# The softmax shift from leading parts: one matmul for four heads, and two buffers for the query rows

## The chip, the cores and the metric

The kernel runs on one core of a Trainium2 chip. The metric is the device time of one execution in microseconds (us). Inputs are float32; on the matrix engine (TensorE, PE) most operands are of type fp32r, a rounded float32 that it streams faster than full float32. A value is therefore often kept as two tiles: a leading part (`h`), which is the value rounded to fp32r, and a rest (`l`), which is the value minus the leading part. The other engines are VectorE (DVE), ScalarE (ACT), GpSimd (POOL), and SyncE (SP), on whose queue nearly all DMAs are issued, in order.

## The reference

For tokens x of shape 2048 x 448, the result mixes an attention branch and an MLP branch with a gate per token:

```python
g = _sigmoid((x * gate_w).sum(-1, keepdims=True))
a = _A_ref(x, A_wq, A_wk, A_wv, A_wo)
b = _B_ref(x, B_w1, B_w2, B_w3, B_w4)
return g * a + (1 - g) * b
```

Branch A is attention with 16 heads of 28 dimensions that share one key and one value (multi-query):

```python
q = (x @ wq).reshape(B, S, H, Dh).transpose(0, 2, 1, 3)
k = x @ wk
v = x @ wv
p = _softmax(jnp.einsum("bhqd,bkd->bhqk", q, k) * (Dh ** -0.5), axis=-1)
o = jnp.einsum("bhqk,bkd->bhqd", p, v)
```

and then the projection with wo. Branch B is a layer norm, a 448 x 448 product with a gelu, shifts along the tokens, a second 448 x 448 product and a residual, and then a layer norm and an MLP of width 1792 with a second residual.

A softmax does not change when one number is taken off all the scores of a row. The kernel uses for it the row's greatest score over the first 128 keys instead of all 2048. This keeps the exponentials in range without being exact; sums above 1e12 would send the kernel into a second, slower pass under a run-time condition at its end.

## The kernel before, in words

**Stages.** The first stage (lines 219 to 376, with its loads) projects keys and values for 4 blocks of 512 tokens, and the queries of the first two units, and does the first half of branch B. The MLP stage (413 to 471) runs 4 blocks of 512 tokens over 14 tiles of the hidden width each, in a loop over `f`. The attention stage (474 on) does the rest of branch A and the gate.

**Units.** The attention goes by 16 units `u = 4 * b + g`: a block of 512 queries and a group of 4 heads. Each unit goes over 16 key tiles `kt` of 128 keys; `k` counts the key tiles of all units. For a key tile there are 4 score matmuls, one for each head (line 683), 4 exponentials (685), and, two key tiles later and for two key tiles at a time, the products with the values (`pv_group`, 645).

**What a score matmul reads.** `kS` holds in its rows 0 to 31 the leading part of the keys, in 32 to 63 the same again, in 64 to 95 their rest, and in rows 96 and on ones. The query rows `qs` hold, for each unit, the leading part of the queries (rows 0 to 31), their rest (32 to 63), the leading part again (64 to 95), and in two rows (96 and 97) the negative shift in two parts. So one matmul over 98 rows gives a score in nearly full precision less its shift.

**How the query rows come about.** A projection of four heads lies in one PSUM tile of 128 rows, row `4 * d + j` for dimension `d` of head `j`. `q_evac` (160) splits it into `qh` (ScalarE, 163) and `ql` (VectorE, 164), and three DMAs on SP (165 to 167) spread these over the rows of `qs`, so that each head has its own 512 columns. Units 0 and 1 are projected in the first stage (`stage_q`), the others by `q_job` (513), two units ahead: its job is put in front of the list at key tile 2 of unit `u - 2` (7 where that is unit 0). There are three buffers for `qs`.

**The shift.** `max_part(u, t)` (177) takes 128 queries of a unit against the first 128 keys: four matmuls of 96 rows, 128 queries and 128 keys (182), one for each head, into one PSUM tile, then one VectorE reduction over it (183). Unit `u + 1` gets its four parts at key tiles 6 to 9 of unit `u`; unit 0 gets them in the MLP stage, in a list of fills. `max_end` and `max_rows` (198, 206) turn the result into the two rows of `qs` with a transposing matmul, a ScalarE copy and two DMAs on SP. `max_full` (185) does it over all keys, for the second pass only.

**What sets the order.** TensorE's order is the order in which the program is written (line 59). The other engines' queues are ordered by a scheduler. In the attention a small pump puts one matmul of a waiting job (projection of queries, normalization, output projection) into TensorE's order after every second score matmul. A normalization job (561) needs the reciprocals of the row sums, which travel by small DMAs on SP (`rt`, 547, and `rb`, 557 and 558).

Of the kernel before, what the change touches and what calls it, by code (L numbers as in the profile page):

```python
# [8 lines left out]
F32 = mybir.dt.float32  # L9
F32R = mybir.dt.float32r  # L10
# [5 lines left out]
P = 128  # L16
# [15 lines left out]
MK = 128  # L32
# [3 lines left out]
def f32(ap):  # L36
    return ap.bitcast(F32)
# [3 lines left out]
def gated_mix_kernel(  # L41
# [13 lines left out]
    nc = tc.nc  # L55

    keep = ctx.enter_context(tc.tile_pool(name="keep", bufs=1))
# [10 lines left out]
    kS = keep.tile([P, S], F32R, name="kS")  # L68
# [4 lines left out]
    first = keep.tile([P, 4], F32, name="first")  # L73
    epst = keep.tile([P, 4], F32, name="epst")
    powt = keep.tile([P, 4], F32, name="powt")
    sel8 = keep.tile([P, P], F32R, name="sel8")
    mcs = [keep.tile([P, P], F32R, name=f"mc_{i}") for i in range(2)]
    nc.gpsimd.memset(epst, EPS)
# [2 lines left out]
    nc.gpsimd.memset(vext, 0.0)  # L81
    nc.gpsimd.memset(vext[:, :, 0:1], 1.0)
    nc.gpsimd.memset(f32(kS)[96:128, :], 1.0)
    nc.vector.tensor_add(
        sel8.rearrange("p (j d) -> p j d", j=4),
        ident[:, 0:4].unsqueeze(2).broadcast_to([P, 4, 32]),
# [36 lines left out]
    def proj32(ps, w, w3, a):  # L123
        for c in range(4):
            nc.tensor.matmul(ps, w(c) if c < 3 else w3, a[:, c, :], start=(c == 0), stop=(c == 3))
# [32 lines left out]
            split_a(tp, ah[:, :, cols], al[:, :, cols])  # L158

    def q_evac(pool, u, ps, qs):  # L160
        qh = pool.tile([P, 512], F32R, tag="qh", bufs=2 if pool.name == "s1" else 1, name=f"qh_{u}")
        ql = pool.tile([P, 512], F32R, tag="ql", bufs=2 if pool.name == "s1" else 1, name=f"ql_{u}")
        nc.scalar.copy(qh, ps)
        nc.vector.tensor_sub(ql, ps, f32(qh))
        nc.sync.dma_start(f32(qs)[0:32], f32(qh))
        nc.sync.dma_start(f32(qs)[32:64], f32(ql))
        nc.sync.dma_start(f32(qs)[64:96], f32(qh))

    NU = NB * NG
    q_of = {}  # L170
    mx_of = {}
    mc_of = {}

    def max_tile(name):
        return psA.tile([P, 512], F32, tag="mx", bufs=1, name=name)

    def max_part(u, t, tile_of):
        if t == 0:
            mx_of[u] = keep.tile([P, 4, 4], F32, tag="mr", bufs=2, name=f"mr_{u}")
        ps = tile_of(f"m_{u}_{t}").rearrange("p (j k) -> p j k", j=4)  # L180
        for j in range(4):
            nc.tensor.matmul(ps[:, j, :], q_of[u][0:96, j, t * P:(t + 1) * P], kS[0:96, 0:MK], start=True, stop=True)  # L182
        nc.vector.reduce_max(mx_of[u][:, :, t], ps, axis=AX.X)  # L183

    def max_full(u, tile_of):
# [33 lines left out]
    with tc.tile_pool(name="s1b", bufs=1) as s1b, \  # L219
            tc.tile_pool(name="ps1", bufs=1, space=PSUM) as ps1:  # L220
        s1_stack = ExitStack()
        s1 = s1_stack.enter_context(tc.tile_pool(name="s1", bufs=1))
# [45 lines left out]
        def stage_kv(b):  # L268
            cols = slice(512 * b, 512 * b + 512)
            ps = max_tile(f"kv_{b}")[0:64, :]  # L270
            if b == 0:
                proj32(ps, lambda c: kvraw[:, c, :], kvlast, xraw[0])
            else:
                ah = s1.tile([P, 4, 512], F32R, tag="ah", bufs=2, name=f"ahk_{b}")
                al = s1.tile([P, 3, 512], F32R, tag="al", bufs=2, name=f"alk_{b}")
                split_a(xraw[b], ah, al)
                proj(ps, kvh, kvl, ah, al)
            nc.scalar.copy(kS[0:32, cols], ps[0:32, :])
            nc.scalar.copy(kS[32:64, cols], ps[0:32, :])
            nc.vector.tensor_sub(kS[64:96, cols], ps[0:32, :], f32(kS)[0:32, cols])  # L280
            vT = s1b.tile([32, 512], F32, tag="vT", bufs=1, name=f"vT_{b}")
            nc.scalar.copy(vT, ps[32:64, :])
            return vT
# [9 lines left out]
        def stage_q(u):  # L293
            ps = mm_tile(f"q_{u}")
            w = slice(u * P, (u + 1) * P)
            proj32(ps, lambda c: wqraw[:, c, w], wqraw[:, 3, w], xraw[0])
            q_of[u] = keep.tile([P, 4, 512], F32R, name=f"qs_{u}", tag=f"qs{u}", bufs=1)
            q_evac(s1, u, ps, q_of[u])

        def ln1_begin(b):  # L300
            ah = s1.tile([P, 4, 512], F32R, tag="ah", bufs=2, name=f"ah1_{b}")
# [48 lines left out]
                    between(t)  # L350

        vT = stage_kv(0)
        stage_q(0)
        stage_v(0, vT)
        stage_q(1)
        ln1_begin(0)
        for t in range(4):
# [116 lines left out]
    with tc.tile_pool(name="s3", bufs=1, reuse_waits="tile") as s3, \  # L474
# [38 lines left out]
        def q_job(u):  # L513
            b, g = divmod(u, NG)
            ah, al = xact[b]
            cols = slice(g * P, (g + 1) * P)
            ps = misc_tile(f"q_{u}")
            ops = []
            for c in range(3):
                ops += [(wqh[:, c, cols], ah[:, c, :]), (wqh[:, c, cols], al[:, c, :]), (wql[:, c, cols], ah[:, c, :])]  # L520
            ops += [(wqh[:, 3, cols], ah[:, 3, :]), (wql[:, 3, cols], ah[:, 3, :])]
            for n, (w, a) in enumerate(ops):
                nc.tensor.matmul(ps, w, a, start=(n == 0), stop=(n == 10))  # L523
                if n < 10:
                    yield
            pool = keep if u % 3 < 2 else s3
            q_of[u] = pool.tile([P, 4, 512], F32R, name=f"qs_{u}", tag=f"qs{u % 3}", bufs=1)
            q_evac(s3, u, ps, q_of[u])
            yield

        rbs = [s3.tile([P, 512], F32R, name=f"rb_{i}") for i in range(2)]
# [83 lines left out]
        for n in range(NT):  # L615
            nc.gpsimd.tensor_scalar(x1[:, n, :], x1[:, n, :], gi[:, n:n + 1], None, op0=ALU.mult)

        jobs = []
        current = [None]

# [45 lines left out]
        for k in range(NU * NT + LAG):  # L666
            u, kt = divmod(k, NT)
            while delayed and delayed[0][0] <= k:
                jobs.append(delayed.pop(0)[1])
            if k == (NU - 1) * NT:  # L670
                for g in range(NG - 2):
                    for t in range(4):
                        jobs.append(lambda t=t, g=g: wo_last_job(t, g))
            if k < NU * NT:
                if kt == (7 if u == 0 else 2) and u + 2 < NU:
                    jobs.insert(0, lambda u=u: q_job(u + 2))
                if kt == 8 and (u + 3) % NG == 0 and u + 3 < NU:
                    load_x((u + 3) // NG)
                p_of[k] = []
                for j in range(4):  # L680
                    n = 4 * k + j
                    ps = s_tile(n, u == NU - 1)
                    nc.tensor.matmul(ps, kS[0:98, kt * P:(kt + 1) * P], q_of[u][0:98, j, :], start=True, stop=True)  # L683
                    p = s3.tile([P, 512], F32, tag="p", bufs=4 * (LAG + PVB) + 2, name=f"p_{n}")
                    nc.scalar.activation(p, ps, AF.Exp, scale=SCALE)  # L685
                    p_of[k].append(p)
                    if j % 2 == 1 or u == NU - 1:
                        pump()
                if u + 1 < NU:
                    if 6 <= kt < 10:  # L690
                        max_part(u + 1, kt - 6, m_tile)
                    elif kt == 10:
                        max_end(u + 1)
                    elif kt == 11:
                        max_rows(u + 1, m_tile)
            if k >= LAG and k % PVB == PVB - 1:
                for kk in range(k - LAG - PVB + 1, k - LAG + 1):
                    if kk >= 0:
                        pv_group(kk)
# [3 lines left out]
        u = NU - 1  # L703
# [50 lines left out]
        with tc.If(again > 0):  # L754
            for b in range(NB):
                load_x(b)
                for g in range(NG):
                    u = b * NG + g
                    for _ in q_job(u):
                        pass  # L760
                    max_full(u, m_tile)
                    max_end(u)
                    max_rows(u, m_tile)
                    pv = max_tile(f"pv2_{u}")
                    for kt in range(NT):
                        for j in range(4):
                            ps = mm_tile(f"s2_{u}_{kt}_{j}")
                            nc.tensor.matmul(ps, kS[0:98, kt * P:(kt + 1) * P], q_of[u][0:98, j, :],
                                             start=True, stop=True)
                            p = s3.tile([P, 512], F32, tag="p", bufs=4 * (LAG + PVB) + 2, name=f"p2_{u}_{kt}_{j}")  # L770
                            nc.scalar.activation(p, ps, AF.Exp, scale=SCALE)
                            nc.tensor.matmul(pv[32 * j:32 * j + 32, :], vext[:, kt, :], p,
                                             start=(kt == 0), stop=(kt == NT - 1), tile_position=(0, 32 * j))
                    for _ in norm_job(u, *recip_begin(u, pv, False)):
                        pass
                for t in range(4):
                    for _ in wo_job(b, t):
                        pass
# [51 lines left out]
```

## Time and profile before

| | before |
|---|---|
| median of 3 runs | 1064.49 us (1064.31 to 1066.27) |
| the profiled execution: its time | 1066.31 us |
| its span | 1064.5 us |
| TensorE busy | 1041.8 us, 98% |
| ScalarE busy | 667.3 us, 63% |
| VectorE busy | 261.7 us, 25% |
| mean granted TensorE clock | 0.992 |

In the profile, `L182` is line 182 of the kernel. PE is TensorE's matmuls, PEld its weight loads, which overlap the matmuls. A row of a group gives busy time, the mean duration of one, and the idle time of the engine just before, with what ended it (`<-`). Matmuls are pipelined, so the duration of one is longer than what it adds to a stream of them. In the chain of waits, which goes back from the last instruction to whatever released it at each step, a matmul is given with the time that it adds. A row of the chain or of a timeline begins with its start and its length in us.

### The profile page before, as it was taken

The numbers are of one execution on the slowest core, as the hardware profiler recorded it, in microseconds if no ns is written. First come the engines' busy times: TensorE is split into PE (matmuls) and PEld (weight loads), VectorE is DVE, ScalarE is ACT, GpSimd is POOL, SyncE is SP. The second block draws the span as 40 slices with busy tenths as digits, with TensorE's granted clock in tenths as the row PEclk, the third lists the DMA queues.
The fourth block names the chain that finished last, engine by engine and source line by source line (L and its number), as shares of the span: only waits on it lengthen the run. The fifth ranks groups of instructions, "written<-read, shape, count | busy, mean of one in ns | idle before, by whom it ended". The sixth has DMA issues, their size and how long they took to land.

```text
span 1064.5 us, 13873 instructions
## 1 busy us (share of the span) xinstructions
PE 1041.8 (98%) x5581; PEld 673.1 (63%) x5581; DVE 261.7 (25%) x540; ACT 667.3 (63%) x1309; POOL 132.6 (12%) x155
## 2 busy tenths in 40 slices
PE   8999899999999999999999999999999999999996
PEld 4687788888888887444554555554655555565542
DVE  6834952411412212311110110120110210111102
ACT  4444451222222224798888888888888889888873
POOL 2422200200200202502000002010002100000100
PEclk9999989999999999999999999999999999999998
DMA  9501330000000002323210202220202220211001
GB/s 306 141 1 38 113 110 1 1 1 1 1 1 1 1 1 75 119 32 71 32 22 11 36 14 40 40 31 3 39 10 41 40 32 2 39 25 26 10 2 38
DMA packets 30653, 41.21 MB, mean 39 GB/s; under 512 B 8116, under 2 KB 20212, under 8 KB 30452
## 3 DMA queue, kind: packets, MB, share of 16 engines
q1 hardware_dynamic: 30356, 40.09, 16.4%
q8 instruction: 46, 0.75, 0.3%
q14 instruction: 27, 0.22, 0.1%
q10 hardware_dynamic: 224, 0.15, 0.0%
HBM read 23.35 MB, written 3.67 MB: 25 GB/s over the span
## 4 chain that ended last, share of the span: by engine, by line
PE 93%; DVE 3%; ACT 1%; POOL 1%; DMA 1%; issue 1%; POOLq 0%; DVEq 0%; SPq 0%; ACTq 0%
PE s L683 27%; PE pv L645 22%; PE acc L439 4%; PE acc L440 4%; PE acc L441 4%; PE g L117 4%; PE g L118 4%; PE g L119 4%; PE q L523 3%; PE m L182 2%; PE wo L580 1%; PE g L121 1%; PE wo L578 1%; PE g L120 1%; PE wo L576 1%; PE h L118 1%
## 5 line engine op out<-in xcount | busy, mean ns | idle before, releaser
L685 ACT ACTIVATE p<-s 128x512 f32<-128x512 f32 x1024 | 517.6, 630 | 99.2 <-PE s L683 98.9
L683 PE MATMUL s<-qs,kS 98*128 98x512 f32 x1024 | 343.4, 420 | 1.4 <-ACT p L685 0.7
L683 PEld LDWEIGHTS s<-qs,kS 98*128 98x128 f32 x1024 | 181.6, 189 | 168.2 <-ACT p L685 127.3
L645 PE MATMUL pv<-p,vext 128*32 128x512 f32 x2048 | 247.6, 602 | 0.0
L429 ACT ACTIVATE gh<-g 128x512 fp32r<-128x512 f32 x56 | 33.5, 598 | 176.7 <-PE g L121 176.7
L645 PEld LDWEIGHTS pv<-p,vext 128*32 128x32 f32 x2048 | 53.7, 109 | 107.8 <-issue 100.4
L431 DVE TENSOR_TENSOR gl<-gf,gh 128x512 fp32r<-128x512 f32 x56 | 38.7, 692 | 185.7 <-ACT gf L430 185.6
L439 PE MATMUL acc<-w4h,gh 128*128 128x448 f32 x224 | 83.4, 372 | 0.0
L440 PE MATMUL acc<-w4l,gh 128*128 128x448 f32 x224 | 81.9, 366 | 0.0
L441 PE MATMUL acc<-w4h,gl 128*128 128x448 f32 x224 | 81.7, 365 | 0.0
L183 DVE TENSOR_REDUCE mr<-m 128x4 f32<-128x512 f32 x64 | 44.3, 691 | 147.4 <-PE m L182 146.7
L117 PE MATMUL g<-ah,w3h 128*128 128x512 f32 x168 | 67.0, 399 | 3.5 <-ACT gf L430 3.5
L119 PE MATMUL g<-ah,w3l 128*128 128x512 f32 x168 | 66.8, 398 | 0.0
L118 PE MATMUL g<-al,w3h 128*128 128x512 f32 x168 | 66.7, 397 | 0.0
L568 POOL CAST onh<-on 128x512 fp32r<-128x512 f32 x15 | 9.2, 614 | 414.4 <-DVE on L565 228.5
L541 DVE SCALAR_TENSOR_TENSOR good<-rt,good 128x16 f32<-128x16 f32 x15 | 2.6, 175 | 190.1 <-DMA rt<-o 190.1
L440 PEld LDWEIGHTS acc<-w4l,gh 128*128 128x128 f32 x224 | 42.4, 189 | 4.7
L439 PEld LDWEIGHTS acc<-w4h,gh 128*128 128x128 f32 x224 | 42.2, 189 | 4.6
L441 PEld LDWEIGHTS acc<-w4h,gl 128*128 128x128 f32 x224 | 42.2, 188 | 3.9
L182 PEld LDWEIGHTS m<-kS,qs 96*128 96x128 f32 x256 | 38.4, 191 | 6.1 <-DVE mr L183 1.2
L117 PEld LDWEIGHTS g<-ah,w3h 128*128 128x128 f32 x168 | 31.9, 190 | 9.9 <-ACT gf L430 3.9
L584 DVE SCALAR_TENSOR_TENSOR ot<-wo,gg,x 128x448 f32<-128x448 f32 x16 | 10.9, 682 | 107.7 <-PE wo L580 107.7
(200 smaller groups left out, 1101.5 us busy)
## 6 DMA issues: line engine op xcount, KB each, us to landing
qs<-qh SPq DMA_DIRECT2D x32, 256.0 KB
qs<-ql SPq DMA_DIRECT2D x16, 256.0 KB
xq<-in_xT_dram SPq DMA_DIRECT2D x4, 1024.0 KB
x<-in_x_dram SPq DMA_DIRECT2D x4, 896.0 KB
w3raw<-in_w_dram SPq DMA_DIRECT2D x7, 512.0 KB
out_dram<-ot SPq DMA_DIRECT2D x16, 224.0 KB
w4raw<-in_w_dram SPq DMA_DIRECT2D x7, 448.0 KB
xkv<-in_xT_dram SPq DMA_DIRECT2D x3, 1024.0 KB
```

Of the source, the lines that this page charges most:

```text
L117: nc.tensor.matmul(ps, wh[:, c, :], ah[:, c, :], start=(c == 0), stop=False)
L118: nc.tensor.matmul(ps, wh[:, c, :], al[:, c, :], start=False, stop=False)
L119: nc.tensor.matmul(ps, wl[:, c, :], ah[:, c, :], start=False, stop=False)
L182: nc.tensor.matmul(ps[:, j, :], q_of[u][0:96, j, t * P:(t + 1) * P], kS[0:96, 0:MK], start=True, stop=True)
L183: nc.vector.reduce_max(mx_of[u][:, :, t], ps, axis=AX.X)
L431: nc.vector.tensor_sub(gl, gf, f32(gh))
L439: nc.tensor.matmul(ps, gh[:, tok], w4h[i][:, k, :], start=(f == 0), stop=False)
L440: nc.tensor.matmul(ps, gh[:, tok], w4l[i][:, k, :], start=False, stop=False)
L441: nc.tensor.matmul(ps, gl[:, tok], w4h[i][:, k, :], start=False, stop=(f == NF - 1))
L645: nc.tensor.matmul(pv[32 * j:32 * j + 32, :], vext[:, kt, :], ps[j], start=(kt == 0), stop=(kt == NT - 1), tile_position=(0, 32 * j))
L683: nc.tensor.matmul(ps, kS[0:98, kt * P:(kt + 1) * P], q_of[u][0:98, j, :], start=True, stop=True)
L685: nc.scalar.activation(p, ps, AF.Exp, scale=SCALE)
```

## The change

The shift is taken from the leading parts of queries and keys alone. A new tile `khd` of 128 rows and 4 x 128 columns is zero but for four blocks: row `4 * d + j` holds in the columns of head `j` the leading part of dimension `d` of the first 128 keys. So `qh` itself, 128 rows by 128 queries, can be the weights of one matmul that streams 512 columns of `khd` and gives the four heads' scores at once, in the place of four matmuls from the query rows. `khd` is zeroed by GpSimd and filled by four DMAs early in the first stage.

As the parts no longer read the query rows, these are needed only when the unit begins. `q_evac` leaves the DMAs to a new `q_rows`, called at the first key tile of the unit before, and two buffers do for `qs`; `qh` gets two buffers in the attention. Unit 1's projection is copied out in full (`q1`) in the first stage, and split and spread at the start of the attention.

```diff
+    khd = keep.tile([P, 4, MK], F32R, name="khd")
+    q1 = keep.tile([P, 512], F32, name="q1")
...
+    nc.gpsimd.memset(f32(khd), 0.0)
...
     def q_evac(pool, u, ps, qs):
-        qh = pool.tile([P, 512], F32R, tag="qh", bufs=2 if pool.name == "s1" else 1, name=f"qh_{u}")
+        qh = (pool if u % 2 else keep).tile([P, 512], F32R, tag=f"qh{u % 2}", bufs=1, name=f"qh_{u}")
+        qh_of[u] = qh
         ql = pool.tile([P, 512], F32R, tag="ql", bufs=2 if pool.name == "s1" else 1, name=f"ql_{u}")
         nc.scalar.copy(qh, ps)
         nc.vector.tensor_sub(ql, ps, f32(qh))
-        nc.sync.dma_start(f32(qs)[0:32], f32(qh))
-        nc.sync.dma_start(f32(qs)[32:64], f32(ql))
-        nc.sync.dma_start(f32(qs)[64:96], f32(qh))
+        ql_of[u] = ql
+        if qs is not None:
+            q_rows(u, qs)
+
+    def q_rows(u, qs):
+        q_of[u] = qs
+        for r, src in enumerate((qh_of[u], ql_of[u], qh_of[u])):
+            nc.sync.dma_start(f32(qs)[32 * r:32 * r + 32], f32(src))
...
         ps = tile_of(f"m_{u}_{t}").rearrange("p (j k) -> p j k", j=4)
-        for j in range(4):
-            nc.tensor.matmul(ps[:, j, :], q_of[u][0:96, j, t * P:(t + 1) * P], kS[0:96, 0:MK], start=True, stop=True)
+        nc.tensor.matmul(ps, qh_of[u][:, t * P:(t + 1) * P], khd, start=True, stop=True)
         nc.vector.reduce_max(mx_of[u][:, :, t], ps, axis=AX.X)
...
-            q_of[u] = keep.tile([P, 4, 512], F32R, name=f"qs_{u}", tag=f"qs{u}", bufs=1)
-            q_evac(s1, u, ps, q_of[u])
+            if u == 0:
+                q_evac(s1, u, ps, keep.tile([P, 4, 512], F32R, name=f"qs_{u}", tag="qs0", bufs=1))
+            else:
+                nc.scalar.copy(q1, ps)
...
         vT = stage_kv(0)
+        for j in range(4):
+            nc.sync.dma_start(f32(khd)[j:P:4, j, :], f32(kS)[0:32, 0:MK])
...
-            pool = keep if u % 3 < 2 else s3
-            q_of[u] = pool.tile([P, 4, 512], F32R, name=f"qs_{u}", tag=f"qs{u % 3}", bufs=1)
-            q_evac(s3, u, ps, q_of[u])
+            q_evac(s3, u, ps, None)
...
+        def qs_tile(u):
+            return (s3 if u % 2 else keep).tile([P, 4, 512], F32R, name=f"qs_{u}", tag=f"qs{u % 2}", bufs=1)
+
+        q_evac(s3, 1, q1, qs_tile(1))
...
+                if kt == 0 and 0 < u < NU - 1:
+                    q_rows(u + 1, qs_tile(u + 1))
```

The second pass, which is not run here, gets its own call of `q_rows`.

More of the change, by code (lines that the diff above doesn't have):

```diff
@@ L164, in q_evac @@
         nc.vector.tensor_sub(ql, ps, f32(qh))
-        nc.sync.dma_start(f32(qs)[0:32], f32(qh))
-        nc.sync.dma_start(f32(qs)[32:64], f32(ql))
-        nc.sync.dma_start(f32(qs)[64:96], f32(qh))
+        ql_of[u] = ql
[5 more added lines that the diff above has]
+            nc.sync.dma_start(f32(qs)[32 * r:32 * r + 32], f32(src))
     NU = NB * NG
     q_of = {}
+    qh_of = {}
+    ql_of = {}
     mx_of = {}
@@ L760, in gated_mix_kernel @@
                         pass
+                    q_rows(u, qs_tile(u))
                     max_full(u, m_tile)
```

## The prediction

> **What bounds the kernel now.** I read the page first (busy shares, the chain that ended last), then the rows of the shift's own tile, then the chain of waits stretch by stretch through the attention.
>
> ```profile
> span 1064.5 us, 13873 instructions
> PE 1041.8 (98%) x5581; PEld 673.1 (63%) x5581; DVE 261.7 (25%) x540; ACT 667.3 (63%) x1309; POOL 132.6 (12%) x155
> ...
> PE s L683 27%; PE pv L645 22%; PE acc L439 4%; PE acc L440 4%; PE acc L441 4%; PE g L117 4%; PE g L118 4%; PE g L119 4%; PE q L523 3%; PE m L182 2%; PE wo L580 1%; PE g L121 1%; PE wo L578 1%; PE g L120 1%; PE wo L576 1%; PE h L118 1%
> ```
>
> TensorE is the bound, and the shift (L182) is itself on the chain, with 2%. What is to be seen next is how much of one attention block it takes. A block here is two key tiles: 16 pv matmuls, 8 score matmuls and whatever fills are pumped between them; it runs from one pv row to the next.
>
> ```profile
> L182 PEld LDWEIGHTS m<-kS,qs x256: 186/192/192, 159.4 to 987.8; 96*128 96x128 f32 x128
> L182 PE MATMUL m<-kS,qs x256: 222/274/328, 159.6 to 987.9; 96*128 96x128 f32 x128
> ```
>
> ```profile
> 505.50 1.85 PE pv L645 x16
> ...
> 510.37 1.85 PE pv L645 x16
> ...
> 513.60 0.23 PE q L523
> 513.83 0.40 PE m L182 x4
> ...
> 515.85 1.85 PE pv L645 x16
> ...
> 553.82 1.85 PE pv L645 x16
> ...
> 558.80 1.85 PE pv L645 x16
> ...
> 567.77 1.85 PE pv L645 x16
> 569.62 2.59 PE s L683 x8
> 572.21 1.85 PE pv L645 x16
> ...
> 625.43 1.85 PE pv L645 x16
> ...
> 631.12 1.85 PE pv L645 x16
> ...
> 636.82 1.85 PE pv L645 x16
> ...
> 641.52 1.85 PE pv L645 x16
> ```
>
> Blocks differ by their fills. With none (567.77) a block takes 4.44 us. With four q matmuls (505.50) it takes 4.87; a q matmul holds the chain for 0.235 (0.23 or 0.24 in single rows), so the block without fills would be 4.87 - 0.94 = 3.93 if TensorE alone set it. The difference, 0.51, is ScalarE:
>
> ```profile
> 565.63 4.03 ACT L685 ACTIVATE p<-s 128x512 f32<-128x512 f32 x8 [0.42 <-PE s L683]
> ```
>
> Eight exponentials take 4.03 and ScalarE waits 0.42 for the first scores, 4.45 together. So a block costs about 3.93 plus fills, and not under 4.45. Every block with shift parts has more: 5.48 (510.37: three q, two parts), 4.98 (553.82: one rbc, two parts), 5.69 (625.43: four q, two parts). There TensorE is the limit, and time taken off the shift comes off the span.
>
> **The change, part by part.**
>
> *Four matmuls become one, in the attention.* From 510.37, a part costs (5.48 - 3.93 - 3 x 0.235) / 2 = 0.42: 0.40 in its row, the rest in the scores behind it. The new matmul loads 128 x 128 weights from the qh tile and streams 512 columns of the block-diagonal tile, the very form of the q matmul: 0.235. Saved: 0.19 a part, 0.38 a block. The new block of three q and two parts is 3.93 + 5 x 0.235 = 5.10. That holds while the block stays above the floor, and one kind comes near: 553.82 becomes 3.93 + 3 x 0.235 = 4.63, where the block of three q and one short transposed row (636.82) took 4.70; I take 0.30 there (ends 0.28 and 0.35). Units 1 to 14 have two such blocks each, 28; followed along the chain, five are of the 553.82 kind and 23 have more fill: 23 x 0.38 + 5 x 0.30 = 10.2. Unit 0 has four parts, but the first ends before a wait for GpSimd (below), so three count: 0.6.
>
> The Trainium skill, page "TensorE: Matmul & The Clock Gate", section "Back-to-back issue gap", gives about 81 ns a matmul at 128 columns and 131 at 512 in a sustained stream of weight load and matmul. By those it would be 4 x 81 - 131 = 193 ns a part, an estimate beside the 0.19 from this trace; the trace's own 100 and 235 ns are what I use. The same section's formula for a lone matmul, N/2.4 + 2.5 ns, speaks against the change, since 512 columns cost the same either way; 4 x 100 against 235 in this trace disagrees with it.
>
> *The shift of unit 0, in the MLP stage.* Its four parts lie in two passes of the f loop.
>
> ```profile
> 154.21 0.60 ACT L429 ACTIVATE gh<-g 128x512 fp32r<-128x512 f32 x1 [1.84 <-PE g L121]
> 159.19 0.60 ACT L429 ACTIVATE gh<-g 128x512 fp32r<-128x512 f32 x1 [3.89 <-PE g L121]
> 165.53 0.60 ACT L429 ACTIVATE gh<-g 128x512 fp32r<-128x512 f32 x1 [5.25 <-PE g L121]
> 171.91 0.60 ACT L429 ACTIVATE gh<-g 128x512 fp32r<-128x512 f32 x1 [5.30 <-PE g L121]
> ```
>
> ```profile
> 160.91 0.69 DVE L183 TENSOR_REDUCE mr<-m 128x4 f32<-128x512 f32 x1
> ```
>
> A pass without fills is 4.98, one with two parts 6.34 and 6.38. The excess of 1.37 is two parts plus a wait: this stage has one PSUM buffer for the parts, the part at 159.6 was reduced only from 160.91, behind the subtraction gl, and the second part waited. In the changed order the first reduction stands ahead of that gl. Two new matmuls add 0.47, so 0.9 a pass, 1.8 in all; if the wait stays, 2 x 2 x 0.19 = 0.8.
>
> *The first stage.* One subtraction of q_1 on VectorE goes.
>
> ```profile
> 19.04 0.68 DVE L164 TENSOR_TENSOR ql<-q,qh 128x512 fp32r<-128x512 f32 x1
> ```
>
> ```profile
> 21.75 1.06 DVE st_s L133 x2
> ...
> 39.31 0.49 PE h L118
> ```
>
> From 21.75 to 39.31 the chain lies mostly on VectorE, so up to 0.5 of the 0.68 arrives. The scheduler also reorders VectorE there: one aggregate and statistics pair moves ahead of the al subtractions. I take 0.5 saved, with ends of 1.3 saved and 1 lost. SP issues four small loads of khd instead of three rows of qs_1, one issue more; behind them stand only the rows of unit 0, first used in the MLP stage or later. The memset of khd on GpSimd falls in its idle time there. The first load of w4 now also waits for the last kv projection, about 2.5 us later than here:
>
> ```profile
> 99.47 0.48 SPq L390 DMA_DIRECT2D w4raw<-in_w_dram  x1
> ```
>
> ```profile
> 107.36 0.92 ACT L391 CAST w4h<-w4raw 128x896 fp32r<-128x896 f32 x1
> ```
>
> Its reader starts at 107.36, so there is cover of some 8 us less the transfer and less 2.5; nothing is charged, a microsecond if the cover fails.
>
> *Start of the attention.* The split of q_1 (one copy, one subtraction, three DMAs) now stands here, and ScalarE's table load moves behind a wait for the first score.
>
> ```profile
> 432.19 3.44 POOL alq L509
> 435.67 0.50 PE q L523
> ```
>
> ```profile
> 412.77 1.28 ACT L685 ACT_TABLE_LOAD   x1
> ```
>
> ```profile
> 423.94 0.92 DVE L600 CAST wqh<-wqraw 128x768 fp32r<-128x768 f32 x1 [4.35 <-DMA wqraw<-in_wq_dram]
> ```
>
> The subtraction falls in VectorE's 4.35 us of waiting, the copy in ScalarE's pause before the scores. The late table load costs up to 1.28 at the first exponential, but TensorE stands waiting for alq until 435.67, some 3.6 us, in any case. So 0; if the cover were gone, 1.3. One of the three row DMAs is put between xq and woraw; if it slowed the loads that alq hangs on, about 1.
>
> *Query rows, moved.* Until now the three row DMAs followed the split at once; now they stand on SP at the first key tile of the unit before, waiting for that buffer's last score, ahead of rt and rb of the reciprocal.
>
> ```profile
> 454.00:455.00 1.00, 1.00 (x14) 0.26 (x8) 0.00 (x0) 1.00 (x4) 0.00 (x0) 1.00 1.12 246
> ...
> 459.00:460.00 1.00, 1.00 (x13) 0.15 (x5) 0.00 (x0) 1.00 (x3) 0.00 (x0) 1.00 0.24 27
> ```
>
> ```profile
> 503.18 0.63 SPq L547 DMA_DIRECT2D rt<-o  x1
> ```
>
> ```profile
> 505.11 0.17 DVE L541 SCALAR_TENSOR_TENSOR good<-rt,good 128x16 f32<-128x16 f32 x1 [21.05 <-DMA rt<-o]
> ```
>
> ```profile
> L558 SPq DMA_DIRECT2D rb<-rl x15: 535/557/697, 468.5 to 1012.8; - x15
> L563 PE MATMUL rbc<-rb,sel x15: 394/397/403, 480.1 to 1025.5; 128*128 128x512 f32 x15
> ```
>
> (The windows' last two columns are the DMA share and GB/s.) One unit's rows keep the DMA engines busy for some 5.2 us. Issued with the unit's first tile, they overlap the landing of rt (1.9 us today) and may delay it by 2 or 3. The first rb is issued 11.6 before its rbc matmul and the last 12.7; less a landing like rt's, 9.7 of slack. Hidden. The rows themselves have a whole unit to land.
>
> Sum: 10.2 + 0.6 + 1.8 + 0.5 = 13.1. The profiled execution took 1066.31 with its span of 1064.5, 1.8 above the median of 1064.49. Taken off the median: 1051.4.
>
> **Rivals.**
>
> *Half the gain.* The parts get shorter but their followers do not: each part's PSUM buffer needs the reduction (0.69) before the next part, or blocks fall on ScalarE's floor. Against it: the parts stand 1.6 us apart and the blocks come out above 4.6. For it: in 553.82 the margin is under 0.2. Keeping half of the 10.8: 1056.8.
>
> *Nothing gained in the attention.* The weight load of 0.19 stands bare in front of the matmul (0.19 + 0.235 = 0.42, what a part costs now), or columns alone are paid. Against it: q's loads are of the same form and hidden. Left are the wait in the MLP stage, 1.37 - 2 x 0.42 = 0.5 a pass, and the first stage's 0.5: 1.5, so 1063.0.
>
> *Slower.* The rows ahead of rt on SP delay the reciprocal past its slack and rbc stalls TensorE in 14 units. It outweighs the gain once rt lands 9.7 + 13.1 / 14 = 10.6 us late, twice what a whole set of rows takes. At 12 us late: 14 x 2.3 = 32 lost, 1083.
>
> **How the numbers follow.** Chances: forecast 0.80 (own range 1049.5 to 1053.5, from the ends of the first stage, the MLP wait and the five short blocks), half 0.12, nothing 0.04, slower 0.04. The range takes in the forecast and the half case, 1049 to 1057. Within 0.2% (2.1 us) counts as no change that a measurement can tell; the nothing case lies inside it: faster 0.92, same 0.04, slower 0.04.
>
> **What would show it.** In the new profile: a shift group of 64 matmuls at 0.235 on the chain; the three-q block at 5.1, the four-q one at 5.3, the rbc one at 4.6 to 4.7, blocks without shift unchanged; passes with parts near 5.45 in the MLP stage; alq still the wait at the start; rbc never waiting for a DMA. A new wait of the shift for its reduction, or of rbc for rb, would make the prediction wrong.

## The result and the profile after

| | before | after |
|---|---|---|
| median, run side by side | 1064.49 us (5 runs, 1062.02 to 1066.91) | 1054.31 us (5 runs, 1053.8 to 1056.95) |
| ratio after to before, 95% interval | | 0.9907 (0.9885 to 0.9928) |
| the profiled execution: its time, its span | 1066.31, 1064.5 | 1055.24, 1053.4 |
| mean granted TensorE clock in it | 0.992 | 0.991 |

The changed kernel is faster by 10.2 us. Forecast were 13.1 less, 1051.4, with a range from 1049 to 1057. So the direction, the stated range and, as will be seen, the main term were right. The narrower range that the prediction gave the forecast itself, 1049.5 to 1053.5, is missed: 2.9 us of the gain are not there. The experiments on the opening of the attention started from them.

The page of the kernel after: its span, the busy time by engine, and the chain that ended last.

```profile
span 1053.4 us, 13462 instructions
PE 1030.6 (98%) x5389; PEld 652.3 (62%) x5389; DVE 263.7 (25%) x540; ACT 667.9 (63%) x1310; POOL 132.3 (13%) x156
...
PE s L702 27%; PE pv L662 23%; PE acc L453 4%; PE acc L454 4%; PE acc L455 4%; PE g L120 4%; PE g L122 4%; PE g L121 4%; PE q L537 3%; PE m L192 1%; PE wo L592 1%; PE wo L590 1%; PE wo L588 1%; PE g L124 1%; PE g L123 1%; PE h L121 1%
```

TensorE is still the bound. There are 192 matmuls fewer, and the shift (now L192) has 1% of the chain instead of 2%. The shift's own rows, and then the chain through two places of the attention, reduced to its pv rows and one shift row (rbc is the broadcast of the reciprocals by a matmul, one of which lies in the block from 513.33):

```profile
L192 PEld LDWEIGHTS m<-khd,qh x64: 187/190/192, 160.1 to 976.0; 128*128 128x128 f32 x64
L192 PE MATMUL m<-khd,qh x64: 387/397/402, 160.3 to 976.2; 128*128 128x512 f32 x64
```

```profile
508.25 1.85 PE pv L662 x16
...
513.09 0.24 PE m L192
513.33 1.85 PE pv L662 x16
...
518.00 1.85 PE pv L662 x16
...
621.24 1.85 PE pv L662 x16
...
626.55 1.85 PE pv L662 x16
...
631.87 1.40 PE pv L662 x9
```

A part holds the chain for 0.23 to 0.24 us. The block of three q and two parts takes 513.33 - 508.25 = 5.08 us (forecast 5.10), the one with rbc 518.00 - 513.33 = 4.67 (4.6 to 4.7), those with four q 5.31 and 5.32 (5.3). From the first pv row of the block at 453.75 before, and 452.26 after, to the last pv row of the loop (1040.38 and 1028.75), before takes 586.63 us and after 576.49: 10.14 less, where units 1 to 14 were put at 10.2.

The MLP stage, by ScalarE's rows for `gh`:

```profile
159.85 0.60 ACT L443 ACTIVATE gh<-g 128x512 fp32r<-128x512 f32 x1 [3.89 <-PE g L124]
165.28 0.60 ACT L443 ACTIVATE gh<-g 128x512 fp32r<-128x512 f32 x1 [4.35 <-PE g L124]
170.75 0.60 ACT L443 ACTIVATE gh<-g 128x512 fp32r<-128x512 f32 x1 [4.39 <-PE g L124]
```

The two passes with parts take 5.43 and 5.47 (6.34 and 6.38 before): 1.82 less, forecast 1.8.

The opening of the attention is another matter. The chain of the kernel after:

```profile
418.09 0.67 ACT L704
...
420.03 5.69 PE s L702 x11
425.72 3.57 PE pv L662 x16
```

ScalarE's table load (the row `ACT L704` at 418.09) has become part of the chain, and the first 16 pv matmuls take 3.57 us instead of 1.85. The windows of four microseconds show why (columns: window; width; busy time and count of PE, PEld, DVE, ACT and POOL; granted TensorE clock; DMA share; GB/s). First after, then before:

```profile
416.00:420.00 4.00, 2.98 (x14) 2.23 (x12) 3.25 (x5) 1.90 (x3) 3.31 (x4) 1.00 0.27 51
420.00:424.00 4.00, 3.97 (x8) 1.64 (x9) 1.35 (x2) 4.00 (x9) 3.85 (x6) 0.92 0.98 358
424.00:428.00 4.00, 4.00 (x16) 1.41 (x19) 3.92 (x5) 3.33 (x7) 3.37 (x3) 0.50 0.74 181
428.00:432.00 4.00, 4.00 (x16) 1.77 (x8) 2.73 (x2) 1.94 (x5) 2.69 (x3) 0.73 0.25 27
```

```profile
420.00:424.00 4.00, 4.00 (x10) 1.53 (x9) 0.06 (x1) 4.00 (x10) 3.85 (x7) 1.00 0.93 351
...
432.00:436.00 4.00, 2.61 (x13) 1.89 (x13) 0.69 (x1) 3.98 (x8) 3.76 (x2) 1.00 0.71 226
436.00:440.00 4.00, 4.00 (x22) 1.02 (x20) 0.69 (x1) 0.04 (x1) 3.85 (x3) 0.57 0.37 116
```

After, TensorE is busy for only 2.98 of the first 4 us (the gap behind the table load), and then its clock is granted at half speed. A window of four us with a clock between 0.50 and 1.00 is read as part of a slow stretch: it holds 8 x (1 - clock) us at 0.50. So the stretch is 0.64 + 4 + 2.16 = 6.8 us long. Before, the same first scores ran at 1.00, TensorE stood at `alq` (the 2.61 of 4.00), and a shorter stretch of 8 x 0.43 = 3.4 us followed.

In the view of the opening used below, from the start of the first score matmul to the start of the sixth group of pv rows, before takes 34.91 us, after 34.58: 0.3 less, where 0.6 was forecast and the waiting for `alq` is gone as well.

### The profile page after: what moved, and what is told of

Its sections match the earlier page's. It is cut to its first block, busy times and chain, and to the rows that moved or that the text cites. A ratio compares the mean times of both kernels' runs of the same rounds, so it can differ in the third digit from the quotient of the medians.

```text
span 1053.4 us, 13462 instructions
## 1 busy us (share of the span) xinstructions
PE 1030.6 (98%) x5389; PEld 652.3 (62%) x5389; DVE 263.7 (25%) x540; ACT 667.9 (63%) x1310; POOL 132.3 (13%) x156
## 4 chain that ended last, share of the span: by engine, by line
PE 93%; DVE 3%; ACT 1%; DMA 1%; POOL 1%; issue 0%; ACTq 0%; SPq 0%; DVEq 0%; POOLq 0%
PE s L702 27%; PE pv L662 23%; PE acc L453 4%; PE acc L454 4%; PE acc L455 4%; PE g L120 4%; PE g L122 4%; PE g L121 4%; PE q L537 3%; PE m L192 1%; PE wo L592 1%; PE wo L590 1%; PE wo L588 1%; PE g L124 1%; PE g L123 1%; PE h L121 1%
## 5 line engine op out<-in xcount | busy, mean ns | idle before, releaser
L704 ACT ACTIVATE p<-s 128x512 f32<-128x512 f32 x1024 | 517.6, 630 | 82.3 <-PE s L702 81.9
L702 PEld LDWEIGHTS s<-qs,kS 98*128 98x128 f32 x1024 | 184.6, 189 | 172.8 <-ACT p L704 136.0
L443 ACT ACTIVATE gh<-g 128x512 fp32r<-128x512 f32 x56 | 33.5, 598 | 175.3 <-PE g L124 175.3
L120 PEld LDWEIGHTS g<-ah,w3h 128*128 128x128 f32 x168 | 31.9, 190 | 10.2 <-ACT gf L444 4.3
L122 PEld LDWEIGHTS g<-ah,w3l 128*128 128x128 f32 x168 | 32.0, 190 | 7.2
```

Source lines behind the costliest of these rows:

```text
L120: nc.tensor.matmul(ps, wh[:, c, :], ah[:, c, :], start=(c == 0), stop=False)
L122: nc.tensor.matmul(ps, wl[:, c, :], ah[:, c, :], start=False, stop=False)
L443: nc.scalar.activation(gh, ps, AF.Gelu_apprx_tanh)
```

## The experiments

Medians are beside the kernel before on the same chip; ratios are to it.

| run | what it changes | median | ratio, 95% interval |
|---|---|---|---|
| rows_only | four matmuls from the rows again, rest as after | 1072.1 | 1.0070 (1.0048 to 1.0093) |
| four_of_khd | four matmuls from `qh` and `khd` | 1064.19 | 1.0000 (0.9986 to 1.0015) |
| two_of_256 | two matmuls of 256 columns | 1053.91 | 0.9901 (0.9878 to 0.9924) |
| rows_four | row DMAs issued four times | 1155.46 | 1.0853 (1.0821 to 1.0884) |
| after_again | the changed kernel | 1054.31 | 0.9904 (0.9889 to 0.9919) |
| early_table | table load ahead of the opening | 1049.6 | 0.9864 (0.9849 to 0.9879) |
| job8 | unit 2's projection a key tile later | 1052.36 | 0.9892 (0.9877 to 0.9907) |
| early_table_job8 | both | 1050.53 | 0.9883 (0.9868 to 0.9898) |
| early_again | early_table, another chip | 1051.89 | 0.9876 (0.9857 to 0.9896) |
| open_filled | idle matmuls in the opening | 1051.35 | 0.9869 (0.9849 to 0.9889) |
| early_filled | early_table and idle matmuls | 1051.02 | 0.9862 (0.9843 to 0.9881) |
| early_job8_filled | all three | 1049.97 | 0.9851 (0.9832 to 0.9870) |

### What a part is paid by

```diff
-        nc.tensor.matmul(ps, qh_of[u][:, t * P:(t + 1) * P], khd, start=True, stop=True)
+        for j in range(4):
+            nc.tensor.matmul(ps[:, j, :], qh_of[u][:, t * P:(t + 1) * P], khd[:, j, :], start=True, stop=True)
```

> The weights and the block-diagonal tile are as changed, but the 512 columns are streamed as four matmuls of 128, each with its own weight load of the same weights. Theory 1, what a part costs is the number of weight loads and matmuls: 0.40 a part as before the change, blocks with three q and two parts at 5.46, time within 2 us of 1064.5. Theory 2, columns are what is paid and the old part was slow through its operands (96 rows, the query rows): 0.235 to 0.28 a part, blocks at 5.1 to 5.2, time near 1054 to 1056.

```diff
-        nc.tensor.matmul(ps, qh_of[u][:, t * P:(t + 1) * P], khd, start=True, stop=True)
+        for j in (0, 2):
+            nc.tensor.matmul(ps[:, j:j + 2, :], qh_of[u][:, t * P:(t + 1) * P], khd[:, j:j + 2, :], start=True, stop=True)
```

> As changed, but two matmuls of 256 columns with one weight load each. Theory 1a, weight loads (0.19 each in their row, some 0.16 apart in a run of four) hide behind matmuls up to 0.235 or so: a part costs about 0.28 to 0.30, a block 5.18 to 5.22, time near 1057. Theory 1b, only columns count once a matmul is as long as 0.117: 0.235 a part, blocks 5.10, time as after the change.

Measured: four matmuls from the new operands give the old time, and two give the new one. The chain of four_of_khd, then that of two_of_256, each through the block of three q:

```profile
509.49 1.85 PE pv L663 x16
...
514.53 0.40 PE m L193 x4
514.93 1.85 PE pv L663 x16
```

```profile
506.41 1.85 PE pv L663 x16
...
511.25 0.24 PE m L193 x2
511.48 1.85 PE pv L663 x16
```

The block takes 5.44 us with four matmuls a part and 5.07 with two; with one it was 5.08. All three stream the same 512 columns. So columns alone are not what is paid (that rival falls), and where the operands come from does not matter. Four matmuls of 128 columns cost 0.40, two of 256 cost 0.235 like one of 512. A weight load takes 0.19 us in the rows of all three, a stream of 256 columns 0.235 / 2 = 0.117. That two such pairs come at the price of their columns, though a load is longer than a stream, was not what I had expected of this run (theory 1a in it); the load is hidden there all the same, and what hides it was not measured further. The formula for a lone matmul, which the prediction weighed from the Trainium skill ("TensorE: Matmul & The Clock Gate", section "Back-to-back issue gap"), would have four of 128 cost about as much as one of 512. The section says itself that it counts too little where the columns are few, and 1064.19 against 1054.31 bears that out here.

### Rows moved, without the new matmul

```diff
-        nc.tensor.matmul(ps, qh_of[u][:, t * P:(t + 1) * P], khd, start=True, stop=True)
+        for j in range(4):
+            nc.tensor.matmul(ps[:, j, :], q_of[u][0:96, j, t * P:(t + 1) * P], kS[0:96, 0:MK], start=True, stop=True)
```

> The four matmuls of 96 rows and 128 columns are put back; everything else stays as changed (two buffers for the query rows, rows at the unit's first key tile, q1 split at the start of the attention). Theory 1, the one matmul carries the gain: a part costs 0.40 on the chain again, the block of three q and two parts is back at 5.46, the one with rbc at 4.97, the one with four q at 5.69; from the second unit on nothing is left of the 10.1 us. In the MLP stage the early reduction still saves part of the wait. Total within 2 us of 1064.5. Theory 2, the moved rows and the freed buffers carry part of it: blocks with parts come out under 5.3 and the time under 1060.

Measured 1072.1, slower than before and outside the 2 us that I had allowed. From unit 1 on the blocks are those of before (5.45 and 4.98), as theory 1 has it, and the two passes with parts in the MLP stage take 6.34 and 6.38 again, so nothing of that wait is saved. The loss lies in the opening, where the block that begins at 448.81 in before begins at 455.59. Its chain, and the row of its waits:

```profile
430.23 0.58 SPq L176
...
430.85 8.58 DMA qs<-qh
...
439.57 1.09 PE m L193 x4
```

```profile
PE m L193 <- DMA qs<-qh: 4.8, 1, 4.8
```

Unit 1's parts read its rows again, and the rows now travel at the start of the attention, two of the three DMAs only at 430 behind the load of `woraw` on SP. Behind the wait of 4.8 us the clock falls a second time (0.89, 0.50 and 0.76 in the windows from 436 to 448, 6.8 us at half), which is part of the loss. So the new matmul has a second effect, which the prediction did not name: because it reads `qh`, unit 1's rows can come so late. The other half, the new matmul with the three row buffers of before, was not run.

### Rows ahead of the reciprocal

```diff
-        for r, src in enumerate((qh_of[u], ql_of[u], qh_of[u])):
+        for r, src in (4 if u > 1 else 1) * list(enumerate((qh_of[u], ql_of[u], qh_of[u]))):
```

> The three row DMAs of each unit from the third on are issued four times over, 12 DMAs ahead of rt on SP; nothing else changes. One set took 5.2 us of all DMA engines, so four take 21, until some 22 us after the unit's start; rt, issued 7 us after it, now lands 1.9 us later. Theory of the prediction (a slack of about 10 us for rt, behind which rbc stalls TensorE): rt lands 14 to 15 us late, rbc waits 3 to 5 us in most of 13 units, 40 to 60 us more than the changed kernel. Rival, rt does not queue behind the rows: no change in the blocks, time as after.

First SP's timeline in the kernel after:

```profile
494.14 0.62 SPq L176 DMA_DIRECT2D qs<-qh  x1
...
495.51 0.60 SPq L176 DMA_DIRECT2D qs<-qh  x1
501.09 0.60 SPq L559 DMA_DIRECT2D rt<-o  x1
```

`rt` is issued at 501.09, when the rows have landed, and its reader starts at 503.0: 1.9 us, as before. The move is hidden, as forecast, and with more room than the 2 or 3 us of delay allowed for. With four sets of rows it is not. The chain of rows_four, in unit 1 and in unit 2:

```profile
454.53 5.43 DMA qs<-ql
...
478.83 0.05 DVEq L168
...
479.63 0.17 DVE good L553
...
484.52 0.77 PE rbc L575
...
524.90 5.43 DMA rt<-o
...
533.80 0.77 PE rbc L575
```

In the second, `rt` takes 5.43 us to land behind the rows, and rbc stands on the chain behind it: the slower rival's mechanism, in its place. In the first, the wait is another one: VectorE's subtraction into the single `ql` buffer (L168) waits for the rows that still read it, and `good`, the reader of `rt`, stands behind it on VectorE. The kernel takes 101 us more, 1155.46 against 1054.31, where I had expected 40 to 60. The waits are not all of it: behind them the clock falls to 0.50, and its mean is 0.949 in this profile, beside 0.991. For the change as made, neither wait exists.

### The opening: table load and alq

```diff
+        e1 = s3.tile([P, 4], F32, name="e1")
+        nc.scalar.activation(e1, q1[:, 0:4], AF.Exp)
         q_evac(s3, 1, q1, qs_tile(1))
```

```diff
-                if kt == (7 if u == 0 else 2) and u + 2 < NU:
+                if kt == (8 if u == 0 else 2) and u + 2 < NU:
```

The first edit is early_table, the second job8.

> The changed kernel once more, as the measure for the three that follow on the same chip. Both theories: 1054.3 within 0.2%. Its opening of the attention (from the first score to the end of the short transposed row of unit 0) took 29.7 us in the first profile; if that is its nature and not chance, it shows again 29.5 to 30.0, with TensorE standing some 1 us behind the late table load and pv rows of about 3.5 us at a granted clock of 0.50 soon after.

> One exponential of four columns of q_1 stands ahead of q_1's split, so that ScalarE loads its table right behind the last gelu and not behind the first score. Theory A (the late table load is what took my 0.6 us at the start of the attention, and 1.28 us more is hidden if it goes): TensorE's gap of 1.05 us behind the first scores and the fall of the clock after it go; TensorE then reaches the q matmul that reads alq before alq is there (434.5), waits some 1 us for it as before, and the clock falls after that gap instead. Opening 28.5 to 29.7, time 0 to 1.2 us less than the changed kernel's. Theory B (the gap costs nothing that would not be lost at alq in any case): opening 29.7 as it is, time the same within 0.3 us. Theory C (the clock fell for another reason than the gap): pv rows of 3.5 us in the same place, opening 28.7.

> Unit 2's projection is started at key tile 8 of unit 0 instead of 7, nothing else: its matmul with alq comes about a block later. In the changed kernel nobody waited for alq any more, so theory A says that this alone gives nothing: opening 29.7, gap behind the first scores and slow pv rows as they are, time the same within 0.3 us. Theory B (alq still bounds the opening, as I predicted): opening 1 us shorter or more.

> Both edits together. Theory A: neither the gap behind the table load nor a wait for alq is left, so TensorE has no gap in the opening and the clock stays at 1.00 there: pv rows of 1.85 throughout, opening 1.05 + 1.72 + 0.3 = 3.1 us shorter (26.6), time 2.5 to 3.3 us less than the changed kernel's, 1051 to 1052. Theory C (the clock falls at the start of the attention whatever the gaps): a slow stretch all the same, opening 28 or more, time at most 1.5 us less.

Measured: the early load gains 4.7 us on the median (1049.6 against 1054.31), with intervals that do not meet; the later job 2.0 and both together 3.8, with intervals that overlap. The 4.7 are more than theory A allowed the table load, and more than the opening shows: in the profiles it got 1.7 us shorter (34.5 to 32.8). The rest lies elsewhere; the part on the prediction shows a place where executions differ by chance. TensorE's gap is gone, but the slow stretch is not. The windows of early_table:

```profile
416.00:420.00 4.00, 4.00 (x16) 2.58 (x14) 2.82 (x5) 2.33 (x5) 3.74 (x5) 1.00 0.41 96
420.00:424.00 4.00, 4.00 (x12) 1.46 (x15) 1.64 (x3) 4.00 (x10) 3.85 (x5) 0.87 0.96 363
424.00:428.00 4.00, 4.00 (x21) 1.41 (x21) 3.96 (x4) 2.10 (x5) 3.37 (x3) 0.70 0.54 131
```

The clock falls at the same place, for 1.04 + 2.4 = 3.4 us instead of 6.8. With both edits there is neither a gap nor a wait for `alq`, and the profiled opening still has 6.8 us at half clock. So theory A (the gap alone makes the fall) falls. job8 alone, for which A expected nothing, shortened the opening from 34.5 to 33.5 us with the same 6.8 us stretch; that is nearly theory B's number, but in the changed kernel nobody had waited for `alq`, and why the opening got shorter was not followed further.

### The opening, filled

The scores of the opening wait for the exponentials to free their PSUM buffers. early_again shows 16 scores in 6.67 us:

```profile
417.58 6.67 PE s L704 x16
424.25 3.10 PE pv L664 x16
```

At 0.235 each TensorE works for 3.76 of these 6.67 us, 56%, and the trace shows no gap between them; a block without fills later in the attention is at 3.93 of 4.45, 88%, and from 440 to 1046 the granted clock of the profiled after is 1.00. Theory D: this thin stretch is the cause, at a moment that a clock of its own decides. The test gives TensorE matmuls whose product nobody reads:

```diff
+        fill_ps = m_tile("fill").rearrange("p (j k) -> p j k", j=4)
...
                     nc.tensor.matmul(ps, kS[0:98, kt * P:(kt + 1) * P], q_of[u][0:98, j, :], start=True, stop=True)
+                    for _ in range(4 if n == 4 else 1 if 4 < n < 16 else 0):
+                        nc.tensor.matmul(fill_ps, identR, khd, start=True, stop=True)
```

(With the early table load one instead of four behind the fifth score, `n == 4`.)

> The early table load once more, beside the kernels with filled openings on the same chip. Theory D, new: the clock falls where TensorE has little to do over some microseconds (in the opening it waits on the exponentials, one score of 0.235 us in about 0.5), at a moment that a clock of its own decides, for 3.4 us or twice that; a gap like that of the table load only makes it likelier. Then the early table load is faster on the median as it was (1049.6, from 1049.3 to 1053.0), with some executions that still have a slow stretch in the opening: median 1049 to 1052. Theory A (the gap alone makes the fall): no slow stretch between 415 and 440 in the profile, and all executions near 1049.5.

> The changed kernel with 15 matmuls more at the start of the attention, whose product nobody reads: four behind the fifth score (they stand in the gap of the table load), one behind each of the next 11. Theory D: no granted clock under 1.00 in the opening, pv rows of 1.85, the opening 29.7 - 1.72 - 0.3 = 27.7 us or, if TensorE then meets alq, up to 1 more; time 1.5 to 2.5 us less than the changed kernel's 1054.3. Theory E (the fall comes from something else at the start of the stage, the DMA loads or the change of work as such): slow stretch as before, time the changed kernel's or up to 1 us more.

> The early table load with 12 such matmuls behind scores 5 to 16. Theory D: no slow stretch in the opening, but TensorE then waits about 1 us for alq at 434.5 where the clock may fall instead; opening 26.9 to 29; time the same as the early table load's good executions, 1049 to 1050.5, without its slow ones. Theory E: slow stretch as before.

> The same, and unit 2's projection begun a key tile later, so that alq isn't waited for. Theory D: no slow stretch anywhere in the opening, which takes some 29.7 - 3.1 = 26.6 us or less; time 1047.5 to 1050. Theory E: slow stretch as before, 1050 to 1051.

The windows of open_filled, then one of early_filled, then the opening chain of early_job8_filled:

```profile
416.00:420.00 4.00, 3.82 (x17) 2.31 (x15) 0.67 (x1) 3.99 (x8) 3.85 (x7) 1.00 0.91 310
420.00:424.00 4.00, 4.00 (x25) 2.08 (x28) 3.79 (x4) 4.00 (x10) 3.92 (x3) 1.00 0.89 266
424.00:428.00 4.00, 4.00 (x28) 1.69 (x24) 3.94 (x4) 3.35 (x8) 2.57 (x2) 1.00 0.06 14
```

```profile
432.00:436.00 4.00, 2.73 (x19) 0.93 (x20) 0.69 (x1) 1.87 (x4) 3.42 (x3) 1.00 1.03 223
436.00:440.00 4.00, 4.00 (x22) 2.65 (x25) 1.35 (x2) 3.68 (x8) 3.92 (x2) 1.00 0.92 273
```

```profile
417.42 1.17 PE s L705 x5
...
424.02 1.85 PE pv L664 x16
```

No slow stretch in the opening of any of the three, and pv rows of 1.85 throughout:

| in the profile | slow stretch in the opening | first score to sixth pv group |
|---|---|---|
| before | 3.4, behind the wait for `alq` | 34.9 |
| after; after_again; two_of_256; job8 | 6.8 in each | 34.6; 34.5; 34.6; 33.5 |
| early_table; early_again; early_table_job8 | 3.4; 3.4; 6.8 | 32.8; 32.8; 32.7 |
| open_filled; early_filled; early_job8_filled | none | 32.8; 32.8; 30.7 |

Theory D holds as far as it goes: filled, the stretch keeps its clock, and in two of three pairs more matmuls make the opening shorter, open_filled by 1.8 us against the changed kernel and early_job8_filled by 2.0 against early_table_job8. In the third, early_filled, the opening stays at 32.8, since TensorE then waits for `alq`. On the whole time this is less clear: the ratio of open_filled is 0.9869, beside 0.9904 for the changed kernel, and the two intervals just touch; early_filled missed its expected range by 0.5 us. Behind its wait for `alq` (2.73 of 4.00 us busy, that is 1.27 us idle) the clock did not fall, where in before it fell behind one of 1.39; these are one profile each, and why they differ is open. Theory E (loads, or the change of work as such) falls. All three edits together take 1049.97, ratio 0.9851 (0.9832 to 0.9870); that is faster than the kernel before, and its interval lies below that of the changed kernel, 0.9889 to 0.9919. It has the lowest ratio of these kernels, though the intervals of the early and filled ones overlap; early_table by itself, with 0.9864 and 0.9876 on two chips, has most of it. Which of these is the fastest, these times do not tell.

## Why the prediction was right, and where 2.9 us went

*Four matmuls become one: right.* 10.14 measured for 10.2, each kind of block within 0.05 us of its forecast, and four_of_khd shows that the four short matmuls, each with its load, were the price: with them the whole gain is gone, within the 1.6 us of the interval, whatever they read. That two of 256 columns are as good as one the prediction did not ask.

*The shift of unit 0: right.* 1.82 for 1.8. The wait for the reduction went with the order on VectorE, as read from it: the first reduction starts at 160.70, ahead of the subtraction `gl` at 161.31. With four matmuls (four_of_khd) it stands behind `gl` again, and the passes take 6.35 and 6.40.

*Rows moved: right.* Hidden with its slack; rows_four shows the two waits that come when the slack is used up. Of these I had named one.

*The first stage: cannot be told.* I took 0.5 as saved. In the profiled execution the first `gh` of the MLP stage starts 0.73 later than before (132.56 against 131.83). Among the 13 profiles with the changed first stage it starts between 130.86 and 132.56, with 131.9 in the middle, and there is one profile of before. So the term is zero within some 0.7 us, and its ends (1.3 saved, 1 lost) held. The load of `w4` kept its cover.

*The start of the attention: the size nearly right, by luck; the mechanism wrong.* The step that failed is "TensorE stands waiting for alq until 435.67, some 3.6 us, in any case. So 0". The chain of waits runs over GpSimd's 3.44 us row there, and I took its length for the length of TensorE's wait. TensorE's own timeline has the wait; first before, then the same matmul after:

```profile
433.66 0.63 PE L683 MATMUL s<-qs,kS 98*128 98x512 f32 x2
435.67 0.50 PE L523 MATMUL q<-alq,wqh 128*128 128x512 f32 x1 [1.39 <-POOL alq L509]
```

```profile
436.47 0.40 PE L537 MATMUL q<-alq,wqh 128*128 128x512 f32 x1
```

It is 1.39 us, just enough for the late table load of 1.28. After, `alq` is ready at 434.46 and its matmul comes at 436.47; nobody waits for it, against my forecast that it stays the wait at the start. And the clock, about which the prediction says nothing, is granted at 0.50 in another place. The starts of the first six groups of pv rows, in us from the first score (TensorE's timeline), show what replaced what:

| | 1 | 2 | 3 | 4 | 5 | 6 |
|---|---|---|---|---|---|---|
| before | 6.41 | 10.85 | 17.75 | 25.05 | 29.97 | 34.91 |
| after | 8.04 | 14.50 | 19.41 | 24.74 | 29.64 | 34.58 |
| open_filled | 7.99 | 12.44 | 17.62 | 22.92 | 27.83 | 32.78 |

To the first group the changed kernel loses 1.6, mostly the table load, and to the second 2.0, the half clock. On the way to the third and the fourth it wins 2.0 each: the wait for `alq`, before's own stretch at half clock, and shorter parts.

The slow stretch is twice as long as before's but not twice as dear, because during much of it TensorE waits for exponentials in any case. Open_filled has none and is 34.58 - 32.78 = 1.8 shorter; before pays 3.47 - 1.85 = 1.6 in its slow pv rows. With these taken off, an estimate, the opening takes 33.3 before and 32.8 after: 0.5 gained at full clock, for the 0.6 forecast. So the fall of the clock is a cost that both kernels pay in their openings, and not what became of the missing 2.9 us.

Where those are can be told in part. Split the profiled pair at the first `gh` of the MLP stage, the first score, the sixth pv group and the last pv row of the loop: the 11.1 us between the two spans are -0.7, 1.9, 0.3, 10.1 and -0.5, where 0.5, 1.8, 0.6, 10.2 and nothing were forecast. So 1.2 of the 2.0 us missing in this pair stand in the first stage and 0.5 at the very end; with one profile of before, it stays open whether the change made them. The other 0.9 is between this pair and the medians.

Executions of the same code differ by more than that, and the profiles show one reason. At the start of the MLP stage TensorE waits for the gelu; in the profile after:

```profile
134.66 0.79 PE L120 MATMUL g<-ah,w3h 128*128 128x512 f32 x1 [3.83 <-ACT gf L444]
```

The wait is 3.5 to 3.9 us long in the profiles of before, after, after_again, job8, early_table_job8 and early_filled. From 132 to 140 the clock is then at 0.50 for 6.8 us in before and after, for 3.4 in after_again and early_filled, and not at all in job8 and early_table_job8, though none of the edits made to the changed kernel touches this place. The first score of the attention comes at 417.6 in after, at 415.5 and 416.3 in the next two, and at 414.3 and 414.6 in the last two. So a median of four or five executions can carry up to 3 us of this by chance, and a part of the 4.7 of early_table may be that.

The mean clock points the same way. On one chip, before (9 executions) and after_again (5) have median spans of 1062.1 and 1052.5; the span times its mean clock, as if TensorE set all of it, has medians of 1056.2 and 1042.9. By this product 13.3 us of work were taken off, against 13.1 forecast, and after lost 9.6 to the clock where before lost 5.9. But the mean also counts the last microseconds of the span, where TensorE has ended and the clock is at 0.50, and stretches in which it waits for others. So the agreement with 13.1 is no proof. The single executions show the spread: after_again took spans from 1049.2 at a clock of 0.994 to 1054.0 at 0.989.

Of the rivals, "half the gain" came nearer in time, 1056.8, 2.5 from the measured median where the forecast is 2.9 away, but not in mechanism: no part waits for its reduction, and no block with parts lies on ScalarE's floor. "Nothing gained" and "slower" are refuted by the blocks. That the result lies in the stated range is owed to this rival, whose time the range took in: the forecast's own range was missed. (The ends that the prediction names for it, 0.8 and 0.25 down, 1.5, 1.0 and 0.1 up, add to 1050.3 to 1054.0, and not to 1049.5 to 1053.5; 1054.31 lies outside either way.)

Open: why the same thin scores did not lower the clock before (16 scores in 6.32 us, and 1.00 until 436) is not settled. That the clock is judged in windows whose phase differs between executions would explain it, and also the start of the MLP stage; no run here sets the phase, and there is one profile of before.

## What to carry to other kernels

A matmul that streams 128 columns behind a weight load of its own costs well over its columns (0.10 us here, where 512 columns cost 0.235): make fewer, wider ones, also through a block-diagonal operand full of zeros, and stop at 256 columns, from where nothing more was gained. Before a wait in the chain is counted as cover, look up in the bounding engine's own timeline how long that engine stood still; the chain's row is the length of the work it waited for. And where the bounding engine starts a stage thinly, look at the granted clock of the microseconds behind it: matmuls whose product nobody reads took 1.8 and 2.0 us off two of three openings here, though on the whole time the intervals overlap or just touch. And where executions of one kernel differ by some us, look for the place in several profiles before a small difference is explained.

## What was not expected of the hardware

The granted clock falls to 0.50 in whole pieces: 3.4 or 6.8 us, in all the openings where it fell. The Trainium skill ("TensorE: Matmul & The Clock Gate", section "What's actually happening") describes a free-running window of 3413 ns that halves the clock after an idle one; the lengths in these traces agree with it, and so does the fall behind the 3.5 to 3.9 us of waiting at the start of the MLP stage, which some executions miss. In the opening its condition, an idle window, does not quite: TensorE was at work for 56% of 6.67 us, without a gap in the kernels with the early table load and with one of 1.05 us in the others, and yet the clock fell in all ten profiles of the changed kernel and its variants whose opening was not filled. Of these, the seven with the late table load (after, after_again, two_of_256, four_of_khd, rows_only, rows_four and job8) had 6.8 us each. At full work, 28 matmuls in 6.7 us or 31 in 8.0, it fell in none of three. Thin work is not enough by itself: in the one profile of before, at 59% of 6.32 us, the clock stayed at 1.00 there.
